# Casting v of row 2, and loading v of row 3, ahead of row 2's dilated scores and of row 3's transposes on SyncE

## Chip, cores, metric

One core of one Trainium2 chip. The metric is the device time of one execution in us. A profiled execution gives a span (first to last instruction) that is some 2 us shorter than its time.

## The reference, cut to what matters

Attention over (batch 8, heads 8, sequence 576, head size 64), then a ReLU-squared MLP. Heads 0 to 3 have a sliding window of 32, heads 4 to 7 a window of 128 in steps of 4 ("dilated").

```python
attn = softmax(where(mask, q @ k.T / 8, -1e9)); a = attn @ v     # per batch row and head
x = a.transpose(0, 2, 1, 3).reshape(4608, 512)
h = x @ w_in; r = maximum(h, 0); out = (r * r) @ w_out
```

A "row" below is one of the eight batch rows. The kernel works on the attention of row b while TensorE also does an MLP chunk (`moe_gen(b - 1)`).

## The kernel before

Each row needs two things from memory. Its q and k are cast to fp16 in DRAM by GpSimd's queue (`dk`), and SyncE then transposes them from there into SBUF (`QKTx` sliding, `QKTd` dilated). Its v is loaded as fp32 by SyncE into one staging buffer (`sv` sliding, `sd` dilated), and ScalarE casts it to fp16 (`vp`, `vd`). There is one staging buffer, so v of row b + 1 can't be loaded before v of row b is cast.

```python
    def load_v(b):
        load_sliding_v(b)                    # six DMAs into sv, SyncE
        load_dilated_v(b, nc.sync)           # two DMAs into sd, SyncE
    def cast_v(eng):
        cast_sliding_v(eng, NB)              # one cast, 1536 columns
        cast_dilated_v(eng, DIL)             # two casts, 1024 columns each
    def keep_qk(b): ...                      # four DMAs on GpSimd's queue: q, k of row b -> dk
    def transpose_by_dma(d): ...             # four DMA transposes on SyncE: dk -> QKTx x2, QKTd x2
    ...
    for b in range(2, B):
        pending.append(moe_gen(b - 1))       # MLP chunk; pump(n) emits n steps of it
        pump(1)
        if 2 < b < B - 1:
            dk = keep_qk(b + 1)
        ...                                  # b == 2: keep_qk(3), weight sums; else pump(11)
        for g in range(2):
            s_sliding_x(b, g)                # scores (ps) and softmax on ScalarE, VectorE
            pump(5)
        s_dilated(b, 0)                      # scores (pz)
        pump(5 if b == 2 else 7)
        s_dilated(b, 1)
        if b + 1 < B:
            transpose_by_dma(dk)
        if b == 2:
            cast_v(nc.scalar)
            load_v(b + 1)
        pump(4 if b == 2 else 9)
        attn_values(b, lambda: pump(2))      # pav, paw, normalize, transposes; the chunk's second half
        if b + 1 < B:
            cast_v(nc.scalar)
        if b + 2 < B:
            load_v(b + 2)
        pump(1000)
```

The scores use a pool of two PSUM buffers, the MLP one of four. ScalarE empties both (L528 `exp`, L290 `relu`).

The softmax here doesn't subtract the row's maximum and nothing guards it: scores larger than these inputs give would overflow.

## Time and profile before

| | before |
|---|---|
| time, median of 3 (range) | 324.56 us (323.42 to 326.12) |
| span of the profiled run | 322.4 us |
| TensorE busy | 295.9 us, 92% |
| row 2, first ps matmul to row 3's first L324 matmul | 24.53 us |
| row 3, first L324 matmul to row 4's | 46.45 us |
| row 4, likewise | 31.19 us |
| clock granted to TensorE at half speed in the middle | 103.65 to 117.3 us |

How to read it: the lines, with those of the order on SyncE and ScalarE, are in the prediction below. L324 is line 324 of the kernel, the first matmuls of an MLP chunk. `ps` and `pz` are the sliding and the dilated scores, `pav` and `paw` their products with v, `ph` the MLP's hidden values and `rt` their ReLU. PE is TensorE, PEld its weight loads, DVE is VectorE, ACT ScalarE, POOL GpSimd and SP SyncE (SPq: its DMA issues). A note such as `[4.56 <-DMA sv<-in_v_dram]` says that the engine had been idle for 4.56 us and what ended that; in a list of waits the numbers are us in total, times, and the longest.

### The profile page before, as it was taken

The numbers are of one execution on the slowest core, as the hardware profiler recorded it, in microseconds if no ns is written. First come the engines' busy times: TensorE is split into PE (matmuls) and PEld (weight loads), VectorE is DVE, ScalarE is ACT, GpSimd is POOL, SyncE is SP. The second block draws the span as 40 slices with busy tenths as digits, with TensorE's granted clock in tenths as the row PEclk, the third lists the DMA queues.
The fourth block names the chain that finished last, engine by engine and source line by source line (L and its number), as shares of the span: only waits on it lengthen the run. The fifth ranks groups of instructions, "written<-read, shape, count | busy, mean of one in ns | idle before, by whom it ended". The sixth has DMA issues, their size and how long they took to land.

```text
span 322.4 us, 7040 instructions
## 1 busy us (share of the span) xinstructions
PE 295.9 (92%) x2920; PEld 196.9 (61%) x2920; DVE 213.5 (66%) x428; ACT 182.9 (57%) x317; POOL 37.4 (12%) x70
## 2 busy tenths in 40 slices
PE   6778999999892199999999999999999999999995
PEld 2767764445781045974696469547954894585484
DVE  5685762789770049767975897589748973844754
ACT  2777974579523367259627952894299336614620
POOL 4340302051003000030004000400010001000000
PEclk9999999999999579999999999999999999999999
DMA  7999899899899939129993998599830003003003
GB/s 186 248 213 246 126 202 242 193 204 304 142 227 292 200 85 177 34 70 237 214 175 119 211 199 168 142 225 193 138 132 0 2 2 130 2 0 133 0 0 132
DMA packets 83312, 47.91 MB, mean 149 GB/s; under 512 B 67792, under 2 KB 79568, under 8 KB 82896
## 3 DMA queue, kind: packets, MB, share of 16 engines
q1 hardware_dynamic: 75060, 26.12, 40.6%
q0 software_dynamic: 6848, 19.80, 27.1%
q10 hardware_dynamic: 1372, 1.54, 1.7%
q8 instruction: 23, 0.38, 0.5%
q14 instruction: 9, 0.07, 0.1%
HBM read 39.85 MB, written 16.52 MB: 175 GB/s over the span
## 4 chain that ended last, share of the span: by engine, by line
PE 64%; DMA 19%; SPq 7%; ACT 6%; issue 2%; POOL 1%; DVE 1%; ACTq 0%; DVEq 0%; POOLq 0%
PE ph L324 27%; PE poa L374 8%; PE pob L374 8%; DMA wi<-in_moe_w_in_dram 5%; DMA sd<-in_v_dram 4%; PE poc L374 4%; PE pod L374 4%; SPq L106 3%; DMA sv<-in_v_dram 3%; DMA dk<-in_k_dram 3%; PE poe L374 3%; DMA sq<-in_k_dram 2%; ACT vp L145 2%; ACT vd L145 2%; PE paw L621 2%
## 5 line engine op out<-in xcount | busy, mean ns | idle before, releaser
L324 PE MATMUL ph<-xT,wi 128*128 128x512 f16 x512 | 119.1, 385 | 13.3 <-ACT rt L290 13.3
L324 PEld LDWEIGHTS <-wi 128*128 128x128 f16 x512 | 48.7, 99 | 70.9 <-issue 17.5
L290 ACT ACTIVATE rt<-ph 128x512 f16<-128x512 f32 x128 | 73.3, 603 | 22.5 <-PE ph L324 22.1
L294 DVE TENSOR_TENSOR g<-rt 128x1024 f16<-128x1024 f16 x56 | 38.7, 691 | 52.0 <-ACT rt L290 51.8
L374 PEld LDWEIGHTS <-sm 128*128 128x128 f16 x512 | 46.9, 98 | 4.9
L374 PEld LDWEIGHTS <-g 128*128 128x128 f16 x384 | 35.8, 98 | 6.5 <-DVE g L292 1.1
L374 PE MATMUL pob<-T,sm 128*128 128x256 f16 x256 | 32.5, 272 | 0.0
L374 PE MATMUL poa<-wo,g 128*128 128x256 f16 x256 | 32.1, 273 | 0.0
L660 ACT COPY xT<-py 128x576 f16<-128x576 f16 x16 | 10.2, 638 | 25.8 <-PE py L654 25.7
L394 POOL DMA_DIRECT2D out_dram<-otl x6 | 4.6, 760 | 174.5 <-DVE otl L429 174.5
L642 ACT COPY xT<-px 128x576 f16<-128x576 f16 x16 | 10.2, 640 | 24.3 <-PE px L636 24.3
L590 DVE TENSOR_TENSOR x_d<-paw,rcp_d 72x512 f16<-72x512 f32 x32 | 22.0, 686 | 1.1
L145 ACT CAST vd<-sd 128x1024 f16<-128x1024 f32 x16 | 16.1, 1051 | 8.6 <-DMA sd<-in_v_dram 8.6
L528 ACT ACTIVATE AT<-pz 128x576 f16<-128x576 f32 x32 | 19.0, 653 | 2.3 <-PE pz L575 1.8
L528 ACT ACTIVATE AT<-ps 128x576 f16<-128x576 f32 x32 | 19.2, 659 | 0.4
L302 PE MATMUL ph<-xT,wi 128*128 128x288 f16 (+1 forms) x128 | 16.8, 272 | 1.8 <-DMA wi<-in_moe_w_in_dram 0.9
L590 DVE TENSOR_TENSOR x_p<-pav,rcp_p 96x512 f16<-96x512 f32 x24 | 16.5, 687 | 0.8
L529 DVE TENSOR_TENSOR AT<-AT,maskp 128x576 f16<-128x576 f16 x32 | 14.5, 457 | 3.8 <-ACT AT L528 2.7
L529 DVE TENSOR_TENSOR AT<-AT,maskd 128x576 f16<-128x576 f16 x32 | 14.2, 463 | 3.3 <-ACT AT L528 2.3
L374 PE MATMUL pod<-T,g 128*128 128x256 f16 x128 | 16.2, 272 | 0.0
L374 PE MATMUL poc<-T,sm 128*128 128x256 f16 x128 | 16.2, 272 | 0.0
L374 PE MATMUL poe<-wo,sm 128*128 128x256 f16 x128 | 16.1, 273 | 0.0
(99 smaller groups left out, 359.3 us busy)
## 6 DMA issues: line engine op xcount, KB each, us to landing
sv<-in_v_dram SPq DMA_DIRECT2D x40, 128.0 KB, 8.2
sd<-in_v_dram SPq DMA_DIRECT2D x7, 512.0 KB, 6.3
dk<-in_k_dram POOLq DMA_DIRECT2D x12, 288.0 KB, 7.9
dk<-in_q_dram POOLq DMA_DIRECT2D x12, 288.0 KB, 8.6
out_dram<-otl POOLq DMA_DIRECT2D x6, 512.0 KB, 3.6
out_dram<-otu POOLq DMA_DIRECT2D x6, 512.0 KB, 5.0
wi<-in_moe_w_in_dram POOLq DMA_DIRECT2D x2, 1024.0 KB, 13.7
wo<-in_moe_w_out_dram POOLq DMA_DIRECT2D x4, 512.0 KB, 10.0
```

Source lines behind the costliest of these rows:

```text
L106: nc.sync.dma_start(out=sv[p0:P, m, :, :], in_=v[b, 0:HH, lo + p0 : lo + P, :].transpose([1, 0, 2]),)
L145: nc.scalar.copy(o, i)
L290: nc.scalar.activation(rt[:, o, :], ph[:], ACTF.Relu)
L294: nc.vector.tensor_mul(g[:, ffc - 1 : ffc + 1, :], rt, rt)
L302: nc.tensor.matmul(ph[:, 0 : t1 - t0], wi[:, dmk, ffc * P : ffc * P + P], xs[:, dmk, :], start=(dmk == 0), stop=(dmk == NDM - 1),)
L324: nc.tensor.matmul(ph, wi[:, dmk, ffc * P : ffc * P + P], xs[:, dmk, :], start=(dmk == 0), stop=(dmk == NDM - 1),)
L374: nc.tensor.matmul(acc, lhs[:, k, t * P : (t + 1) * P], rhs[:, k, :], start=(first and k == 0), stop=(k == NK - 1), skip_group_check=True,)
L528: nc.scalar.activation(AT[:, u, 0:UW], ps[:, :, 0 : UW // 2], ACTF.Exp, scale=scale)
L529: nc.vector.tensor_mul(AT[:, u, 0:UW], AT[:, u, 0:UW], mask)
L590: nc.vector.tensor_tensor(out=x[0:w], in0=pv[:, :, :, 0:D], in1=rcp[0:w].unsqueeze(3).to_broadcast([w, 2, HH, D]), op=ALU.mult,)
L642: nc.scalar.copy(xT[:, 0:2, t0 : t0 + 288], px[:, 0:UW].rearrange("x (c t) -> x c t", c=2),)
L660: nc.scalar.copy(xT[:, 2:4, t0 : t0 + 288].rearrange("x c (i r) -> x c i r", r=DIL), py[:, 0:UW].rearrange("x (c r i) -> x c i r", c=2, r= ...
```

## The change

The intent is to have row 3's v in SBUF before ScalarE comes to its casts. For that row 2's casts, which free the staging, go ahead of row 2's dilated scores, and row 3's load of v goes ahead of row 3's transposes in SyncE's stream.

```diff
         for g in range(2):
             s_sliding_x(b, g)
             pump(5)
+        if b == 2:
+            cast_v(nc.scalar)
+            load_v(b + 1)
         s_dilated(b, 0)
         pump(5 if b == 2 else 7)
         s_dilated(b, 1)
         if b + 1 < B:
             transpose_by_dma(dk)
-        if b == 2:
-            cast_v(nc.scalar)
-            load_v(b + 1)
         pump(4 if b == 2 else 9)
```

## The prediction

> **What bounds the kernel now.** I read the page first: TensorE is busy 92% of the span, but slices 13 and 14 of its row read 2 and 1, the only hole after the start. So the kernel is bound by TensorE, except in that hole. Next the busy time of each engine in stretches, cut where a row of the batch starts its first L324 matmul (row 3, row 4, row 5):
>
> ```profile
> 95.23:141.68 46.45, 33.76 (x319) 21.48 (x317) 23.54 (x45) 20.36 (x34) 3.16 (x6) 0.85 0.64 145
> 141.68:172.87 31.19, 31.03 (x319) 20.78 (x316) 23.54 (x45) 19.81 (x34) 3.50 (x6) 1.00 0.90 180
> 172.87:204.06 31.19, 31.03 (x318) 20.80 (x316) 23.53 (x45) 19.81 (x34) 3.50 (x6) 1.00 0.90 180
> ```
>
> Columns: length, then busy us of PE, PEld, DVE, ACT, POOL, then granted clock, DMA share and GB/s. Rows 4 and 5 take 31.19 us each with TensorE busy 31.03: they have no slack. Row 3 does the same work (319 matmuls) in 46.45 us, that is **15.26 us more**, at a mean clock of 0.85. Who waits there, from the waits between 64 and 147 us:
>
> ```profile
> PE ph L324 <- ACT rt L290: 12.8, 2, 12.7
> ACT vd L145 <- DMA sd<-in_v_dram: 8.6, 2, 5.6
> ACT vp L145 <- DMA sv<-in_v_dram: 4.6, 1, 4.6
> ```
>
> TensorE waits for ScalarE to empty a PSUM buffer, and ScalarE itself waits for v. The timeline gives the order:
>
> ```profile
> 82.87 5.66 SPq L194 DMA_TRANSPOSE QKTx<-dk  x2
> 88.63 2.71 SPq L196 DMA_TRANSPOSE QKTd<-dk  x2
> 91.44 3.25 SPq L106 DMA_DIRECT2D sv<-in_v_dram  x6
> 94.79 2.30 SPq L113 DMA_DIRECT2D sd<-in_v_dram  x1
> 97.19 0.68 SPq L114 DMA_DIRECT2D sd<-in_v_dram  x1
> ...
> 98.87 1.47 ACT L145 CAST vp<-sv 128x1536 f16<-128x1536 f32 x1 [4.56 <-DMA sv<-in_v_dram]
> ...
> 103.28 1.04 ACT L145 CAST vd<-sd 128x1024 f16<-128x1024 f32 x1 [2.93 <-DMA sd<-in_v_dram]
> 109.94 1.04 ACT L145 CAST vd<-sd 128x1024 f16<-128x1024 f32 x1 [5.62 <-DMA sd<-in_v_dram]
> ...
> 111.53 3.57 PE L324 MATMUL ph<-xT,wi 128*128 128x512 f16 x8 [12.69 <-ACT rt L290]
> ```
>
> SyncE queues the four transposes of row 3 ahead of row 3's v. The transposes cannot go before row 3's dk has landed (82.7 us; the waits of SyncE's queue give 12.3 us of it in one piece). So v is issued from 91.44 on, its last part lands at 109.9, and the casts that stand in ScalarE's stream ahead of the L290 of that row hold up TensorE for 12.69 us. The rest of the 15.26 is the clock: TensorE is busy 33.76 - 31.03 = 2.73 us longer for the same matmuls.
>
> **What the Trainium skill says.** "TensorE: Matmul & The Clock Gate", Part 1 (the HAM clock gate): an idle TensorE drops to half clock after an idle window of about 3.4 us and needs about as long of busy work to get it back. The trace agrees in kind: idle from 98.85, clock 1.00 until about 103.7, 0.50 until about 117.3, nearly 6 us after work resumed. "DMA: Bandwidth & Descriptors", Anatomy of one DMA: DMA engines don't wait on semaphores, the wait is on the issuing sequencer before dispatch. So a transpose that waits for dk holds v behind it on SyncE; the trace shows just that. Same page, Queues, rings and completion order (arbitration): an engine goes round its rows packet by packet. This bears on sharing with dk, whose packets are large: between 103 and 107 us the GpSimd queue moved 0.74 MB and SyncE's queue 0.03 MB although sd was still incomplete. "ScalarE: Activation LUTs", What ACT_TABLE_LOAD costs: 186 ns + 0.833 ns per element, 1.47 us for 1536 and 1.04 us for 1024 columns; the casts took 1.47 to 1.48 and 1.04 to 1.05, so they cost the same wherever they stand.
>
> **The change, part by part.** Nothing is added or removed; the built order shows three ScalarE casts, two groups of SyncE issues and 32 score matmuls (buffer names alone) in another place.
>
> (1) The casts of row 2's v move from behind row 2's last exp to ahead of its first dilated exp. ScalarE before:
>
> ```profile
> 75.00 1.24 ACT L290 ACTIVATE rt<-ph 128x512 f16<-128x512 f32 x2
> 76.32 1.19 ACT L528 ACTIVATE AT<-pz 128x576 f16<-128x576 f32 x2
> 77.40 1.09 ACT L290 ACTIVATE rt<-ph 128x512 f16<-128x512 f32 x2
> 78.71 0.60 ACT L290 ACTIVATE rt<-ph 128x512 f16<-128x512 f32 x1 [0.22 <-PE ph L324]
> 79.20 1.19 ACT L528 ACTIVATE AT<-pz 128x576 f16<-128x576 f32 x2
> 80.26 1.48 ACT L145 CAST vp<-sv 128x1536 f16<-128x1536 f32 x1
> 81.62 2.01 ACT L145 CAST vd<-sd 128x1024 f16<-128x1024 f32 x2
> ```
>
> The casts would start at 76.25. Row 2's v is there by then, just: its last load was issued at 70.00 and took 5.7 us, so it landed at 75.7. They take ScalarE 83.52 - 80.26 = 3.26 us. Everything between (two exps, three L290, two exps) moves back by 3.26, less the 0.22 us of idle time that it absorbs: about 3.0. Does TensorE feel it? Yes. The second pair of dilated score tiles, written at 78.60 before, needs the two PSUM buffers that the first pair's exps free, now at about 80.2 and 80.8 instead of 77. That is a wait of about 2 us. Behind it, ffc 12 to 15 come late by 3.0, then VectorE's L294, L292, four sums (2.5 us), two masks and the normalize of the first pav: before, that normalize ended at 84.00 and the third pav matmul, which takes its buffer, started at 84.05. There is no slack in this chain, so that matmul comes 3.0 us late. The 0.91 us for which pav waited for the cast vp before lies inside the same interval and so doesn't come off. **Cost on the path: 3.0 us.** From there on (84.05 to 98.85) TensorE had no idle time, so it stays.
>
> (2) Row 3's v is loaded as soon as the casts have read the staging: sv from 77.75 (when the vp cast ends), sd by about 82, 13.7 us earlier than before. Until dk has landed at about 82.5 these packets will trickle. Then sv (0.74 MB) and sd (0.8 MB) at the 0.2 MB/us that such loads ran at alone take about 7.5 us: landed at about 90. They are needed when ScalarE reaches row 3's casts, 94.3 before and 97.3 after. **Slack about 7 us, so the wait for v goes, with its slow clock: 15.26 us removed**, row 3 then taking 31.19 like its successors.
>
> (3) The transposes now stand behind these loads, in SyncE's stream, and wait for the first four sv pieces to land too (the built program's waits show one DMA counter of eight shared by each). Issue shifts from 82.87 to about 84, but their data lie behind sd in the ring: 84.3 to 92 before, about 90 to 98 after. Row 3's sliding scores ran 5.6 us after a row's start in row 4 (147.27 against 141.68), hence at 98.2 + 5.6 = 103.8. Hidden. Row 4 and later see the same order as before.
>
> Sum: 324.56 - 15.26 + 3.0 = **312.3 us**, 3.8% faster.
>
> **Rivals.** (a) *The wait only changes place*: v collides with dk, or the transposes come too late, so that row 3's scores wait. For it: DMA engines are at a share of about 1 from 64 to 80 and from 84 to 112, and dk starves the other queue. Against it: the share is 0.79 and 0.10 at 80 to 84, a hole which the earlier v fills; and 6 us of slack at both ends. It would give 313 to 318. (b) *ScalarE pays more*: if row 2's v lands after 76.25 in other runs, each us blocks exps and L290 and goes on the path at once; or the pieces of idle time between 78.6 and 87 (about 4 us in all) drop the clock, as the 12.69 us did. Against it: the pieces are 1 to 2 us, with work between. It would give 314 to 316. (c) *The casts cost nothing*: VectorE catches up and only the PSUM wait of about 2 us less the old 0.91 stays: 310.5. (d) *It was hidden anyway*: against it stands row 3's 46.45 against 31.19; I give it nearly nothing.
>
> **Range and chances.** The centre is 312.3. Rival (c) sets the low end, 310.5; (b) and the mild form of (a) the high end, 315.0. The three runs of before span 0.8%, which is within this. Faster by 2% means under 318.1: only a strong form of (a) misses it. Chances: faster 0.94, within 2% 0.05, slower 0.01.
>
> **What would show it right or wrong.** Right: no wait of L145 for sv or sd in row 3; PE's wait for ACT rt of 12.69 us gone, and the clock 1.00 from row 2 to row 7; row 3 31.2 us from first L324 to first L324; row 2's casts at about 76.3 and about 3 us of new idle time on TensorE between 78.6 and 87, in front of pz, poa and pav; SyncE's L194 at about 84 and row 3's ps matmuls without a wait. Wrong: ps in row 3 waiting for QKTx (rival a), the vd cast of row 2 waiting for sd (rival b), or row 2 as long as before (rival c).

## The result, and the profile after

| | before | after |
|---|---|---|
| time, median (range) | 325.13 us, 4 runs (323.42 to 326.12) | 312.21 us, 4 runs (311.64 to 312.40) |
| ratio, 95% interval | | 0.9605 (0.9559 to 0.9651) |
| row 2 / row 3 / row 4 | 24.53 / 46.45 / 31.19 us | 27.53 / 30.87 / 31.19 us |

Ratios, here and below, are the mean time of one kernel's fast runs over that of the other's fast runs of the same rounds, so not quite the ratio of the medians quoted.

Busy time by stretch of the changed kernel (length; busy us of PE, PEld, DVE, ACT, POOL; clock; DMA share; GB/s), for rows 2, 3 and 4:

```profile
71.46:98.99 27.53, 25.67 (x284) 18.69 (x284) 21.16 (x43) 16.73 (x27) 3.33 (x7) 0.94 1.12 229
98.99:129.86 30.87, 30.87 (x318) 20.80 (x316) 23.53 (x45) 19.06 (x34) 3.14 (x6) 1.00 0.96 188
129.86:161.05 31.19, 31.03 (x318) 20.79 (x316) 23.53 (x45) 19.82 (x34) 3.49 (x6) 1.00 0.88 180
```

Row 3 lost its 15 us (46.45 to 30.87, 15.58 us less), and row 2 became 3.0 us longer. The timeline of SyncE after:

```profile
78.38 7.39 SPq L106 DMA_DIRECT2D sv<-in_v_dram  x6
85.86 0.42 SPq L113 DMA_DIRECT2D sd<-in_v_dram  x1
86.38 0.38 SPq L114 DMA_DIRECT2D sd<-in_v_dram  x1
86.95 8.51 SPq L194 DMA_TRANSPOSE QKTx<-dk  x2
95.56 2.72 SPq L196 DMA_TRANSPOSE QKTd<-dk  x2
```

v now goes first, and its last piece took 5.8 us to land (92.2). ScalarE comes to row 3's casts at 97.97 and finds it there: these two lines have no idle time noted behind them, where the three of before had 4.56, 2.93 and 5.62 us.

```profile
97.97 1.48 ACT L145 CAST vp<-sv 128x1536 f16<-128x1536 f32 x1
99.35 1.99 ACT L145 CAST vd<-sd 128x1024 f16<-128x1024 f32 x2
```

So the time and the two main terms came out as predicted. Whether for the reason given is another question. In the kernel before, the last piece of sd took 12.7 us from issue to landing, and only 5.8 now. The order on SyncE says when v is issued; it doesn't say why it then takes twice as long. The experiments take this apart.

### The profile page after: what moved, and what is told of

It is laid out like the page before. It is cut to its first block, busy times and chain, and to the rows that moved or that the text cites. A ratio compares the mean times of both kernels' runs of the same rounds, so it can differ in the third digit from the quotient of the medians.

```text
span 310.6 us, 7040 instructions
## 1 busy us (share of the span) xinstructions
PE 295.0 (95%) x2920; PEld 197.2 (63%) x2920; DVE 213.5 (69%) x428; ACT 182.5 (59%) x317; POOL 37.3 (12%) x70
## 4 chain that ended last, share of the span: by engine, by line
PE 75%; DMA 11%; ACT 7%; SPq 2%; issue 2%; DVE 1%; POOL 0%; ACTq 0%; DVEq 0%
PE ph L324 31%; PE poa L374 9%; PE pob L374 9%; DMA wi<-in_moe_w_in_dram 6%; PE pod L374 5%; PE poc L374 4%; PE poe L374 3%; DMA sv<-in_v_dram 3%; ACT vd L145 3%; ACT vp L145 3%; DMA sq<-in_k_dram 2%; SPq L106 2%; PE paw L621 2%; PE pav L607 2%; PE ph L302 2%
## 5 line engine op out<-in xcount | busy, mean ns | idle before, releaser
L324 PE MATMUL ph<-xT,wi 128*128 128x512 f16 x512 | 116.5, 379 | 0.6 <-ACT rt L290 0.6
L324 PEld LDWEIGHTS <-wi 128*128 128x128 f16 x512 | 48.1, 98 | 56.4 <-issue 1.8
L374 PE MATMUL poa<-wo,g 128*128 128x256 f16 x256 | 33.4, 278 | 0.2 <-DVE g L294 0.2
L345 PE MATMUL po<-wo,g 128*128 128x512 f16 x64 | 16.1, 379 | 0.0
```

The lines of the kernel that those rows point to most:

```text
L324: nc.tensor.matmul(ph, wi[:, dmk, ffc * P : ffc * P + P], xs[:, dmk, :], start=(dmk == 0), stop=(dmk == NDM - 1),)
L345: nc.tensor.matmul(po, g[:, ffc, t * P : (t + 1) * P], wo[:, ffc, :], start=(ffc == 0), stop=(ffc == NFF - 1),)
L374: nc.tensor.matmul(acc, lhs[:, k, t * P : (t + 1) * P], rhs[:, k, :], start=(first and k == 0), stop=(k == NK - 1), skip_group_check=True,)
```

## The experiments

Twelve runs of ten new kernels (e9 is the changed kernel and e10 is e5 once more), all correct. "Row 2" and "row 3" are the lengths read off each profile's timeline, between the same matmuls as above.

| run | row 2 | row 3 | median us (range, runs) | ratio to before |
|---|---|---|---|---|
| before | 24.53 | 46.45 | 324.56 (323.42 to 326.12, 3) | |
| the change | 27.53 | 30.87 | 312.21 (311.64 to 312.40, 4) | 0.9605 |
| e1 casts early, v behind | 27.26 | 34.38 | 315.75 (315.39 to 318.51, 4) | 0.9727 |
| e2 v ahead, casts late | 24.52 | 43.65 | 325.19 (321.06 to 329.99, 4) | none given |
| e3 the change, GpSimd casts | 27.45 | 30.87 | 311.44 (311.09 to 311.46, 4) | 0.9573 |
| e4 the change, wait filled | 27.27 | 30.88 | 311.57 (311.11 to 312.10, 4) | 0.9580 |
| e5 e2, dk of row 4 held | 24.52 | 30.88 | 309.03 (308.95 to 310.54, 4) | 0.9563 |
| e6 before, dk of row 4 held | 24.52 | 40.45 | 318.20 (317.88 to 318.68, 4) | 0.9832 |
| e7 e2, row 2 slower | 26.46 | 49.58 | 319.72 (318.52 to 329.47, 4) | 0.9865 |
| e8 before, row 2 slower | 26.47 | 37.67 | 317.50 (316.17 to 318.34, 4) | 0.9805 |
| e9 the change again | 27.26 | 30.87 | 311.72 (311.26 to 312.39, 6) | none given |
| e10 e5 again | 24.52 | 31.25 | 311.88 (308.95 to 316.61, 6) | none given |
| e11 the change, dk held | 27.26 | 30.87 | 312.02 (311.06 to 313.11, 6) | none given |
| e12 e2, stores and dk held | 24.52 | 30.87 | 308.91 (308.37 to 310.15, 6) | 0.9524 |

The medians of before in the rounds of e1 to e4, e5 to e8, e9 to e11 and e12 were 325.49, 323.75, 324.72 and 325.01. Two of e2's runs (328.25, 329.99), two of e10's (314.10, 316.61) and one of e7's (the profiled one, 329.47) were over 1.5% above the fastest of their kernel and so count as slow; ratios leave them out, and I draw nothing from them but that these kernels scatter. The medians in the table include them. Of e2 too few fast runs are left for a ratio: its two fast ones took 321.06 and 322.13. The lengths of rows in e7 are those of its slow, profiled run. The intervals of e6 (0.9799 to 0.9865), e7 (0.982 to 0.991) and e8 (0.9763 to 0.9848) lie under 1, so each is faster than before; for e6 and e8 it isn't settled whether by 2%, and for e7 it is less. In the rounds of e9 to e11 one run of before took 318.16, by which its ten others (323.71 to 325.89) count as slow, so no ratio is given there, and I compare the three with each other.

### e1: the casts early, v still behind the transposes

Against the changed kernel:

```diff
         if b == 2:
             cast_v(nc.scalar)
-            load_v(b + 1)
         s_dilated(b, 0)
 ...
             transpose_by_dma(dk)
+        if b == 2:
+            load_v(b + 1)
```

> Row 2's casts early as in the changed kernel, but row 3's v loaded behind the transposes as before. My theory (the gain is that v no longer stands behind transposes that wait for dk; the early casts are a pure cost): v is issued at about 91 to 92 again, the wait of L145 for sd and the 12 us hole come back; the 3 us that the casts cost in row 2 are swallowed by the hole, as v's arrival doesn't depend on TensorE. Ratio to before 0.995 to 1.005, about 325 us. Rival (the gain comes from casting early, which empties the staging): 312 to 316 us, ratio below 0.975.

My theory fell. With v behind the transposes, exactly as before, and issued even a little later (from 93.68 us, before 91.44), 9.7 us of the gain were there. ScalarE's timeline in row 3 of e1:

```profile
100.85 1.47 ACT L145 CAST vp<-sv 128x1536 f16<-128x1536 f32 x1 [3.10 <-DMA sv<-in_v_dram]
102.78 1.04 ACT L145 CAST vd<-sd 128x1024 f16<-128x1024 f32 x1 [0.46 <-DMA sd<-in_v_dram]
104.03 1.05 ACT L145 CAST vd<-sd 128x1024 f16<-128x1024 f32 x1 [0.20 <-DMA sd<-in_v_dram]
```

The long waits for sd, 2.93 and 5.62 us, are gone. Its last piece was issued at about the same time as before and landed in half the time.

### e2: v ahead of the transposes, the casts at their old place

Against the kernel before:

```diff
-        if b + 1 < B:
-            transpose_by_dma(dk)
         if b == 2:
             cast_v(nc.scalar)
             load_v(b + 1)
+        if b + 1 < B:
+            transpose_by_dma(dk)
```

> Row 2's casts at their old place (behind row 2's last dilated exps); only the load of row 3's v is put ahead of the transposes. My theory (the order on SyncE gives the whole 15.3 us, the early casts cost 3.0 us): v issued from about 81.8, landed by 92 to 93, casts of row 3 at about 94.5 to 98 without a stall over 1 us, clock 1.00 throughout: 309.2 us, ratio to before 0.952, that is 3 us under the changed kernel. Rival (the early cast is needed, as the transposes issued behind v now come too late for row 3's scores, which stand at about 101, or v is late): ps waits for QKTx or L145 for sd in row 3, 311 to 316 us, ratio 0.958 to 0.975.

This fell too, and it is the other half of the surprise: the order on SyncE alone, which I had credited with everything, took 2.80 us off row 3 in the profiled run. The two fast runs (321.06 and 322.13) are on average 3.7 us under the mean of before, and the two slow ones are above every run of before in these rounds. v was on time in the profiled run, which is a fast one (landed at 93.8, no wait of L145 in row 3), and row 2 took 24.52 us. But the wait had moved to the transposes. First a line of e2's waits, then its DMA queues and issues from 102 to 108 us (queue: packets, MB, share of 16 engines; issue: us to landing):

```profile
PE pz L575 <- DMA QKTd<-dk: 10.7, 1, 10.7
```

```profile
q1 hardware_dynamic: 194, 0.05, 101.7%
q0 software_dynamic: 12, 0.10, 11.6%
...
QKTd<-dk SPq DMA_TRANSPOSE x1, 18.0
```

The time that the packets of SyncE's queue (q1) took adds up to the whole time of 16 engines (101.7%), and they moved 0.05 MB in 6 us; in e12 below, where it is alone, the same queue moved 1.35 MB from 97 to 103 us. A QKTd transpose took 18.0 us to land. What else was under way: GpSimd had issued row 2's last stores at 95.47 and 97.30 and row 4's dk from 98.01. That gave the new theory. **SyncE's traffic (transposes and v of row 3) has to be through before GpSimd's traffic (stores of row 2, dk of row 4) begins, and GpSimd's begins when TensorE ends row 2.** The kernel before loses the last piece of sd in this collision, e2 the last transpose. The early casts help e1 and the changed kernel by holding TensorE up for 3 us, so that GpSimd starts 3 us later.

### e3: the change, with the casts on GpSimd

Against the changed kernel:

```diff
-            cast_v(nc.scalar)
+            cast_v(nc.gpsimd)      # the early cast of row 2
```

> The changed kernel, but with row 2's casts on GpSimd, which is idle then. From GpSimd's cast of 512 columns at the start (657 ns) I estimate 2.0 + 1.3 + 1.3 = 4.6 us for the three. My theory (the 3.0 us of row 2 are ScalarE's time in front of the dilated exps): row 2 takes 23.6 to 24 us instead of 27.5, no clock drop, 308.3 us, ratio to before 0.950. Rival (the 3 us come from DMA traffic or from the loads, not from ScalarE): no better than the changed kernel, 311.5 to 313.

Row 2 stayed at 27.45 us although ScalarE no longer had the casts ahead of its exps. VectorE's timeline says why; these are two sums that take 0.69 us elsewhere:

```profile
73.73 3.43 DVE L280 TENSOR_TENSOR sm<-sm,g 128x1024 f16<-128x1024 f16 x1
77.09 1.52 DVE L281 TENSOR_TENSOR sm<-g 128x1024 f16<-128x1024 f16 x1
```

GpSimd cast from 74.12 to 78.06, and VectorE lost 3.6 us in just that time ((3.43 - 0.69) + (1.52 - 0.69)). The Trainium skill, "GPSIMD Engine Reference", section 1 (Specifications), says that GpSimd's SBUF interfaces are shared with VectorE, with contention for VectorE instructions that have two SBUF inputs, as these have; this trace agrees. So the cost moved from ScalarE to VectorE, and the run doesn't settle what I built it for: both theories failed to name this.

### e4: one MLP step moved into TensorE's wait

Against the changed kernel:

```diff
-        pump(5 if b == 2 else 7)
+        pump(6 if b == 2 else 7)
         s_dilated(b, 1)
 ...
-        pump(4 if b == 2 else 9)
+        pump(3 if b == 2 else 9)
```

> The changed kernel, but one step of the MLP (four poa matmuls, 0.44 us) moved from behind the second pair of dilated scores to ahead of it, into TensorE's wait there. If the third pav matmul was held by the clock drop of 83.1 to 86.5, this takes part of the idle time out and may keep the clock up: row 2 shorter by 0.3 to 1 us, 311.2 to 312. If it was held by VectorE's chain as I predicted: no change within 0.3 us, 312.2.

The run tells apart what held up the third pav matmul in row 2. In the changed kernel's profile the clock was at half from 83.05 to 86.47 us, and TensorE did not wait for VectorE. In e4 there was no clock drop, pav waited 1.19 us for VectorE, and row 2 was no more than 0.26 us shorter. e1 and e9, which have the same row 2 as the changed kernel and had no drop either, show the same 27.26 us and the same wait. From the waits of e9:

```profile
PE pav L607 <- DVE x_p L590: 1.2, 1, 1.2
```

So VectorE's chain is the limit, as predicted. A clock drop covers that wait: in the changed kernel's profile it added 0.27 us, and in e11's (half clock from 81.5 to about 84.6 us, row 2 again 27.26) nothing. As e1 and e9 had no drop either, its absence in e4 can't be credited to the filled wait, and the time of e4 can't be told from e9's.

### e5 to e8: the collision, prevented and postponed

e5 is e2, and e6 is the kernel before, with row 4's dk held back: GpSimd reads one column (an element per partition) of what has to land first. In e6 `pump(1000)` only brings row 2's last stores ahead of that read; the order of each engine's other work stays.

```diff
 # e5, ahead of keep_qk(4)
+        if b == 3:
+            for i in range(2):
+                nc.gpsimd.tensor_copy(hold, QKTx[:, i, PADP + HH * S - 2 : PADP + HH * S - 1])
+                nc.gpsimd.tensor_copy(hold, QKTd[:, i, 1, KPAD + S - 1 :])
 # e6, after row 3's cast_v, ahead of load_v(4) and keep_qk(4)
+        if b == 2:
+            pump(1000)
+            for i in range(2):
+                nc.gpsimd.tensor_copy(hold, sd[:, i, 0, 0:1])
```

> The swap alone (e2, 325.2 us), with one thing more: GpSimd reads one element of each of row 3's transposes before it issues the loads of row 4's dk, so these can't run beside the transposes. My new theory (what decides is whether SyncE's transposes and loads of v are through before GpSimd's stores and dk of the next row start; in e2 the QKTd transposes took 18 us to land beside them): the 10.7 us wait of pz for QKTd goes, row 2 stays at 24.5 us, 309 to 312 us, ratio to before 0.95 to 0.96. Rival (in e2 the transposes are late by their own length and their place behind v, dk has no part): about as e2, over 320 us.

> The kernel before, with row 4's dk held until row 3's dilated v has landed; the order of casts, v and transposes is untouched. New theory (of the 12.7 us hole of before a good part is the last piece of sd, starved for some 6 us by dk): sd lands at about 104 instead of 109.9, the hole shrinks to 6 to 8 us, 317.5 to 320.5 us. Theory of the prediction (v is late because it stands behind transposes that wait for dk of row 3, and no more): 325 us, unchanged.

e7 is e2, and e8 the kernel before, with useless work on TensorE in row 2:

```diff
+        if b == 2:
+            pf = pmool.tile([P, TOKC], FP32, name="pf", tag="pm")
+            idle_matmuls(pf, 14, TOKC)
         attn_values(b, lambda: pump(2))
```

> The swap alone (e2), with 14 idle matmuls of 512 columns (3.0 us) on TensorE ahead of row 2's attention values: nothing but a later TensorE, and with it later stores and later dk of row 4. New theory (the collision is a question of when GpSimd's queue starts): the wait for QKTd shrinks or goes, so that 3 us of added useless work make the kernel faster than e2: 311 to 318 us. Rival (the early cast does something of its own): e2 plus 3 us, 328 us.

> The kernel before, with the same 3.0 us of idle matmuls ahead of row 2's attention values. New theory (casting early helped e1 only by holding TensorE up for 3 us, so that v had landed when stores and dk of row 4 began): as e1, 314.5 to 317.5 us, ratio about 0.973, sd's last piece landed at about 104. Rival (the early cast frees the staging, or ScalarE, and that is what helped): 325 to 328 us.

Three of the four are clear. e5: with dk held, the swap alone takes 308.95 to 310.54 us instead of e2's 321.06 to 329.99 (another chip; e10 below, on e2's chip, has 308.95 to 316.61); row 3 is 30.88 us. e6: with nothing changed but the start of dk, the kernel before gains 5.6 us (medians); its row 3 is 6.0 us shorter. e8: adding matmuls that compute nothing makes the kernel before *faster* by 6.3 us. They delayed row 2 by 1.94 us, not by 3.0, mostly since the 0.91 us that pav waited for its cast passed beside them; so 317.5 is at the end of what I expected. The same piece of sd (512 KB), issued at 97.0 to 97.6, from issue to landing in the DMA issues of before, e6, e8 and e1, one fence each:

```profile
sd<-in_v_dram SPq DMA_DIRECT2D x1, 512.0 KB, 12.7
```

```profile
sd<-in_v_dram SPq DMA_DIRECT2D x1, 512.0 KB, 7.6
```

```profile
sd<-in_v_dram SPq DMA_DIRECT2D x1, 512.0 KB, 6.6
```

```profile
sd<-in_v_dram SPq DMA_DIRECT2D x1, 512.0 KB, 6.4
```

And TensorE's hole in row 3, from the waits of e6 and of e8 (before 12.7):

```profile
PE ph L324 <- ACT rt L290: 8.0, 2, 7.8
```

```profile
PE ph L324 <- ACT rt L290: 5.2, 2, 5.1
```

GpSimd's first store after row 2, in the timelines of before and of e8 (in e1 it is at 98.31):

```profile
94.88 0.77 POOL L394 DMA_DIRECT2D out_dram<-otl  x1 [21.18 <-DVE otl L429]
```

```profile
96.44 0.77 POOL L394 DMA_DIRECT2D out_dram<-otl  x1 [19.93 <-DVE otl L429]
```

For v the theory can be narrowed from dk and stores to dk. From 97 to 103 us GpSimd's queue (q0) was busy beside SyncE's (q1) in e8 too:

```profile
q1 hardware_dynamic: 1417, 0.96, 52.6%
q0 software_dynamic: 216, 0.82, 38.5%
```

The packets of q0 were 3.8 KB on average, which fits the stores (issued first, 1 MB in all), and sd still landed in 6.6 us. In the kernel before, from 103 to 107 us, they were 9.3 KB on average (0.74 MB in 80 packets), which fits dk, and SyncE's queue moved 0.03 MB. e6, in which dk alone was held and the stores ran beside v, agrees (7.6 us). So v may run beside the stores; what it must escape is dk. That the packets are those of the stores and of dk is inferred from their size and from the order of issue.

e7 is a partial miss. Its three fast runs were 318.5 to 320.3, a little under e2's fast 321.06 and 322.13 but above my 311 to 318, and the profiled one was 329.47, with pz waiting 15.8 us for QKTd. It seems that a delay of 1.9 us isn't enough to clear the transposes, which are behind v there and end later; but the only trace is that of the slow run, so this isn't shown for the fast ones.

### e9 to e12: is there a version that beats the change?

e9 is the changed kernel, e10 is e5, e11 is the changed kernel with e5's hold on dk, all on one chip.

> The changed kernel once more, on the same chip and in the same rounds as the next two, to compare them directly: 312.2 us, ratio to before 0.960.

> The kernel of e5 once more (swap without the early casts, row 4's dk held behind row 3's transposes). If the early casts are a cost of 3 us once the collision with dk is prevented otherwise: 309.1 us, 3.0 us and 1.0% under the changed kernel of the same rounds. If e5's lead was the chip's or the day's: within 1 us of it.

> The changed kernel, with row 4's dk held behind row 3's transposes as in e5. In the changed kernel the transposes had landed before dk's packets came, so there is nothing left to prevent: 312.2 us, within 0.5 us of the changed kernel. If some collision was left in it: under 311.5.

e11 equals e9 (312.02 and 311.72): holding dk gains nothing in the changed kernel. e10 showed that e5's 309.03 is not safe: 308.95 to 316.61, and the mean of its fast runs, 310.74, is only 1.0 us under e9's 311.73. In e5 and e10 only dk is held; row 2's stores still run beside the last transposes. So in e12 GpSimd waits ahead of the stores:

```diff
 # e2, behind the transposes
+        if b == 2:
+            for i in range(2):
+                nc.gpsimd.tensor_copy(hold, QKTx[:, i, PADP + HH * S - 2 : PADP + HH * S - 1])
+                nc.gpsimd.tensor_copy(hold, QKTd[:, i, 1, KPAD + S - 1 :])
         pump(4 if b == 2 else 9)
```

> The swap alone (e2), with GpSimd held until row 3's transposes have landed before it issues row 2's last stores, and so row 4's dk too (in e5 and e10 only dk was held, and the stores still ran beside the transposes; e10's times spread from 308.95 to 316.6). If the spread of e10 came from the stores: 308.5 to 310 us in all runs, spread under 1.5 us, a version that beats the changed kernel by 2 to 3 us. If it came from the late transposes themselves (they end near 102 to 105, row 3's scores need them from 100.7 on): spread and median as e10, 309 to 316.

All six runs lie between 308.37 and 310.15, ratio 0.9524 (0.9492 to 0.9557). GpSimd's timeline in e12:

```profile
102.26 0.18 POOL L828 CAST hold<-QKTd 128x1 f32<-128x1 f16 x1 [1.96 <-DMA QKTd<-dk]
...
103.51 0.77 POOL L394 DMA_DIRECT2D out_dram<-otl  x1 [0.45 <-issue]
104.27 0.73 POOL L394 DMA_DIRECT2D out_dram<-otu  x1
104.98 0.54 POOL L184 DMA_DIRECT2D dk<-in_k_dram  x1
```

The stores go 8 us later than in e2 and nobody misses them. The QKTd transposes landed in 3.7 us in e12, and beside the stores in 5.6 in e10's profiled run and 7.3 in e5's. e12 beats the changed kernel by about 3 us: its row 2 is back at 24.52, its row 3 at 30.87. The two ran on different chips, each against the kernel before there, and their intervals only just don't overlap (0.9492 to 0.9557, 0.9559 to 0.9651), so the size of the lead is less sure than its sign.

## Why the prediction was right, and where it was not

- **Row 3 loses 15.26 us**: right (15.58). No wait of L145 for v, no wait of TensorE for rt in the middle of the row, clock 1.00 there. "The clock 1.00 from row 2 to row 7" did not hold in the profiled run, by the drop in row 2 below.
- **Row 2 pays 3.0 us**: right (3.0 in the profiled run, 2.74 in e1, e4, e9 and e11). The steps are those predicted: pz waited 1.43 and 0.23 us for the exps, then the third pav for VectorE's chain (1.19 us in e1, e4 and e9; in the changed kernel's own profile the half clock took the place of this wait). That the clock may drop (rival b) happened in the profiled run of the change, and in e11's, and cost 0.3 us at most.
- **The early casts as a cost on the path**: right once the collision is prevented by other means. e5 and e12 have the casts at the old place and row 2 at 24.52 us, row 3 at 30.88 and 30.87.
- **Transposes**: "Issue shifts from 82.87 to about 84" was off: SyncE was at 86.95, as issuing the six sv took it 7.39 us. They landed by about 102, not 98, and the dilated scores of row 3 ran at 109.5: hidden, as said. v landed at 92.2 instead of 90, so the slack was 5.8 us and not 7.
- **The cause in step (2) was incomplete, and this is the failure.** It read: v issued 13.7 us earlier, "Slack about 7 us, so the wait for v goes, with its slow clock: 15.26 us removed", as though the order on SyncE were all of it and the casts in (1) a pure cost. The runs show that, with the casts early, the place ahead of the transposes gives 3.5 us of row 3 (e1's 34.38 to 30.87). The other 12.07 us (46.45 to 34.38) came with the early casts alone. They delayed TensorE, and through it GpSimd's stores and dk, so that dk's packets hardly met v (its last piece landed in 6.4 us and not 12.7). (The split depends on the order: the swap first gives 2.80 us, e2.) That it was the delay is shown by e8, where matmuls without use and no early cast brought row 3 to 37.67. The 3.29 us that e8 still lacks to e1 are accounted for by the profiles: TensorE waited 5.07 us for rt and not 3.35, and the L324 matmuls after it took 3.46 us at half clock and not 1.89. Net of the 2.73 us that row 2 pays, the early casts gave 9.3 us. Without that delay the swap would have run into rival (a): that is e2, with row 3 at 43.65 us. So the number came out partly by luck: the 3 us that the prediction booked as a cost were what kept rival (a) away. I had named rival (a), and set it aside with slacks computed for the changed kernel, whose 3 us delay was part of them. The line that should have warned me is among those I looked at: an sd of 512 KB that took 12.7 us to land, when such loads needed 5.7 in row 2.

What stays open: why dk and DMA transposes slow each other as far as they did in e2, where both nearly stood still from 102 to 108 us; and whether stores were what slowed e10's slow runs, which have no trace (e12's narrow spread fits, it doesn't show it).

## What to carry to other kernels

Before moving a load forward, look at when the *other* queues start, and at what triggers them: a faster stage also starts its successors' transfers earlier, and these can hit the transfer that you moved. A transfer's time from issue to landing, compared with the same transfer in a quiet row, tells a late issue from a collision. And undo each half of a change by itself: here either half alone would have taught the wrong lesson, and the hold that prevents the collision (a few columns read on the issuing engine) beat the change that avoided it by being slow.

## What the Trainium skill lacked or had wrong

- "DMA: Bandwidth & Descriptors": it has the round-robin by packet, but no figure for what this costs a stream of small packets or DMA transposes beside large DRAM-to-DRAM ones. Here a 512 KB load went from 6.4 to 12.7 us, and a QKTd transpose from 3.7 to 18.0 us; SyncE's queue moved 0.05 MB in 6 us.
- "TensorE: Matmul & The Clock Gate": its closing rule speaks of idle gaps over about 3 us. The page does say elsewhere (A second HAM failure mode) that many short idle pieces can do the same, but gives no size for them. In the changed kernel the clock dropped at 83.05 though no piece of idle time was longer than 1.43 us, in two (the change, e11) of the four profiles with the same gaps in row 2 (e1 and e9 had no drop).
